# Decode attention with a dense block: a scheduled kernel of two load queues written anew as a looped program of one

## The chip, the cores and the metric

One core of one Trainium2 chip. The metric is device time in microseconds (us): the median of three runs, beside one profiled execution of the same program. PE is TensorE, DVE is VectorE, ACT is ScalarE, POOL is GpSimd, SP is SyncE; a name such as SPq stands for the engine's instruction queue. Matrix products in float32 are recorded as two passes each, so one matmul of the program is two records.

## The reference, cut to what matters

```python
B, D, H, Sk, Dh, F = 2, 512, 32, 8192, 128, 1792       # one new token for each of two sequences, float32

q = (layernorm(x) @ wq).reshape(B, 1, H, Dh)
scores = einsum("bhqd,bhkd->bhqk", q, k_cache) * Dh ** -0.5
o = einsum("bhqk,bhkd->bhqd", softmax(scores), v_cache)
h = x + o.reshape(B, 1, H * Dh) @ wo
r = relu(layernorm(h) @ w1 + b1)
out = h + (r * r) @ w2 + b2
```

There are 64 pairs of a head and a sequence. Each pair has 4 MiB of K and 4 MiB of V, and each of those bytes is used once. wq and wo have 8 MiB each, w1 and w2 3.5 MiB each.

## The kernel before

The host lays the data out so that each transfer is one row for each of the 128 partitions. K is laid with the head dimension on the partitions and the 8192 keys along the row, in two chunks (`NC`) of four quarters (`NQ`) of 1024 keys (`CS`). V is laid with 32 of the head's columns in each of four groups of partitions, so that the partition 32j + m holds quarter j, and four tiles (`NH`) of 1024 keys cover the 128 columns.

A pair has two chunks, and one chunk t goes through two steps. `front(t)`: eight matmuls (line 154) put the scores of 4 x 1024 keys into a tile `s` in PSUM, four at a time in four column groups of the array, with q repeated 32 times as the weights; DVE takes the negated maximum of each partition (line 156); ACT overwrites the scores with their exponentials and sums them (line 158). `back(t)`: DVE multiplies the exponentials with each of four tiles of V and sums along the row (line 166), writing the products themselves to a scratch tile `junk`.

The pairs lie in ten groups of heads (`GROUPS`, 4 heads down to 1). Each group has its own load of wq and wo, a projection of its q (`project_q`, line 140), a correction of its partial maxima and sums (`weigh`), and a joining step that multiplies with wo and adds into `hT` (`combine`, lines 195 to 208). At the end stand the second layer norm (`centre`), the products with W1 (line 252) and W2 (line 266), and the store.

The order of the instructions is the order in which the program calls them, two chunks ahead (`AHEAD`), and a tile framework puts in the waits: a load waits until the tile's last use is over. K, wq, wo, W1 and W2 are issued by SP (lines 57, 63, 68, 228, 232), V by ACT (line 73, and line 77 for the last but one pair); the last pair's V is issued by SP in eight pieces (line 80). There are three K tiles and two V tiles of 4 MiB (32 KiB in each partition). The loop over chunks is unrolled: 7969 instructions are in the trace.

Of the kernel before, what the change touches and what calls it, by code (L numbers as in the profile page):

```python
# [1 line left out]

# [9 lines left out]
AX = mybir.AxisListType  # L12

# [6 lines left out]
GROUPS = [4] * 7 + [2, 1, 1]  # L20
HEAD0 = [sum(GROUPS[:g]) for g in range(len(GROUPS))]
NG = len(GROUPS)
# [4 lines left out]
T = BH * NC  # L27
TH = B * NC
AHEAD = 2
W2_PIECES = [4, 4, 3, 2, 1]  # L30
# [4 lines left out]
@with_exitstack  # L35
def attention_block_kernel(ctx: ExitStack, tc: tile.TileContext, small, kd, vd, wqd, wod, w1d, w2d, out):
    nc = tc.nc
    consts = ctx.enter_context(tc.tile_pool(name="consts", bufs=1))
    kp = ctx.enter_context(tc.tile_pool(name="kp", bufs=3))
    vp = ctx.enter_context(tc.tile_pool(name="vp", bufs=2))  # L40
    wts = ctx.enter_context(tc.tile_pool(name="wts", bufs=2))
    work = ctx.enter_context(tc.tile_pool(name="work", bufs=2))
    ps_s = ctx.enter_context(tc.tile_pool(name="ps_s", bufs=3, space=bass.MemoryType.PSUM))
    ps_m = ctx.enter_context(tc.tile_pool(name="ps_m", bufs=2, space=bass.MemoryType.PSUM))


    sm = consts.tile([P, DB * B + FB + DB], F32, name="sm")
# [4 lines left out]
    KT, VT, WQ, WO = {}, {}, {}, {}  # L52

    def load_wq(g):
        n = P * DB * DH
        WQ[g] = wts.tile([P, DB, GROUPS[g] * DH], F32, name="wq")
        nc.sync.dma_start(WQ[g].rearrange("p d c -> p (d c)"),
                          wqd[HEAD0[g] * n : (HEAD0[g] + GROUPS[g]) * n].rearrange("(p x) -> p x", p=P))

    def load_wo(g):  # L60
        n = P * D
        WO[g] = wts.tile([P, GROUPS[g], D], F32, name="wo")
        nc.sync.dma_start(WO[g].rearrange("p h c -> p (h c)"),
                          wod[HEAD0[g] * n : (HEAD0[g] + GROUPS[g]) * n].rearrange("(p x) -> p x", p=P))

    def load_k(i):
        KT[i] = kp.tile([P, NC, NQ, CS], F32, name="k")
        nc.sync.dma_start(KT[i], kd[i])

    def load_v(i):  # L70
        VT[i] = vp.tile([P, NC, NH, CS], F32, name="v")
        if i < BH - 2:
            nc.scalar.dma_start(VT[i], vd[i])
            return
        for c in range(NC):
            if i < BH - 1:
                nc.scalar.dma_start(VT[i][:, c], vd[i][:, c])
            else:
                for e in range(NH):
                    nc.sync.dma_start(VT[i][:, c, e], vd[i][:, c, e])  # L80


    ones_d = consts.tile([P, P], F32, name="ones_d")
    nc.vector.memset(ones_d, 1.0 / D)
    eps_t = consts.tile([P, 1], F32, name="eps_t")
    nc.vector.memset(eps_t, EPS)
    zero = consts.tile([P, 1], F32, name="zero")
    nc.vector.memset(zero, 0.0)
    pick = consts.tile([P, NQ, P], F32, name="pick")
    nc.vector.memset(pick, 0.0)  # L90
    pick_all = consts.tile([P, P], F32, name="pick_all")
    nc.vector.memset(pick_all, 0.0)
    for j in range(NQ):
        nc.vector.memset(pick[32 * j : 32 * j + 1, j, :], 1.0)
        nc.vector.memset(pick_all[32 * j : 32 * j + 1, :], 1.0)
    ident = consts.tile([P, P], F32, name="ident")
    make_identity(nc, ident)
    fold = consts.tile([P, 32], F32, name="fold")
    nc.vector.tensor_reduce(fold, ident.rearrange("p (j m) -> p m j", j=NQ), axis=AX.X, op=ALU.add)

    def mean(src):

        part = work.tile([P, B], F32, name="part")
        nc.vector.tensor_reduce(part, src.rearrange("p d b -> p b d"), axis=AX.X, op=ALU.add)  # L104
        pm = ps_m.tile([P, B], F32, name="pm")
        nc.tensor.matmul(pm, ones_d, part, start=True, stop=True)  # L106
        return pm

    def centre(src):

        xc = work.tile([P, DB, B], F32, name="xc")
        nc.vector.tensor_tensor(xc, src, mean(src)[:, None, :].to_broadcast([P, DB, B]), op=ALU.subtract)
        sq = work.tile([P, DB, B], F32, name="sq")
        nc.vector.tensor_tensor(sq, xc, xc, op=ALU.mult)
        rstd = work.tile([P, B], F32, name="rstd")
        nc.scalar.activation(rstd, mean(sq), AF.Sqrt, bias=eps_t, scale=1.0)
        nc.vector.reciprocal(rstd, rstd)
        return xc, rstd

    load_wq(0)  # L120
    nc.sync.dma_start(sm, small)
    load_k(0)
    xn = consts.tile([P, DB, B], F32, name="xn")
    xc, rstd = centre(xT)
    nc.vector.tensor_tensor(xn, xc, rstd[:, None, :].to_broadcast([P, DB, B]), op=ALU.mult)
    hT = consts.tile([P, DB, B], F32, name="hT")
    nc.vector.tensor_copy(hT, xT)
    warm = consts.tile([P, 1], F32, name="warm")
    nc.scalar.activation(warm, eps_t, AF.Exp)


    QR, NM, LS, AC, PT, WS, RL = {}, {}, {}, {}, {}, {}, {}
    where = [(g, (hl * B + b), c) for g in range(NG) for hl in range(GROUPS[g]) for b in range(B) for c in range(NC)]

    def project_q(g):
        nb = GROUPS[g] * B
        pq = ps_m.tile([P, nb], F32, name="pm")
        for hl in range(GROUPS[g]):
            for d in range(DB):
                nc.tensor.matmul(pq[:, hl * B : (hl + 1) * B], WQ[g][:, d, hl * DH : (hl + 1) * DH], xn[:, d, :],  # L140
                                 start=(d == 0), stop=(d == DB - 1))
        QR[g] = work.tile([P, nb, 32], F32, name="qr")
        nc.vector.tensor_scalar(QR[g], pq[:, :, None].to_broadcast([P, nb, 32]), SCALE, None, op0=ALU.mult)  # L143
        NM[g] = work.tile([P, nb, NC], F32, name="nm")
        LS[g] = work.tile([P, nb, NC], F32, name="ls")
        AC[g] = work.tile([P, nb, NC, NH], F32, name="ac")

    def front(t):

        g, i, c = where[t]  # L150
        s = ps_s.tile([P, CS], F32, name="s")
        for n in range(CS // 512):
            for j in range(NQ):
                nc.tensor.matmul(s[32 * j : 32 * j + 32, n * 512 : (n + 1) * 512], QR[g][:, i, :],  # L154
                                 KT[t // NC][:, c, j, n * 512 : (n + 1) * 512], start=True, stop=True)
        nc.vector.tensor_reduce(NM[g][:, i, c : c + 1], s, axis=AX.X, op=ALU.max, negate=True)  # L156
        PT[t] = s
        nc.scalar.activation(s, s, AF.Exp, bias=NM[g][:, i, c : c + 1], scale=1.0,  # L158
                             accum_out=LS[g][:, i, c : c + 1])

    def back(t):

        g, i, c = where[t]
        for e in range(NH):
            junk = consts.tile([P, CS], F32, name="junk")
            nc.vector.scalar_tensor_tensor(junk, VT[t // NC][:, c, e, :], 1.0, PT[t], op0=ALU.mult, op1=ALU.mult,  # L166
                                           accum_out=AC[g][:, i, c, e : e + 1])

    def weigh(g):

        nb = GROUPS[g] * B
        pn = ps_m.tile([P, NQ, nb, NC], F32, name="pm")
        for j in range(NQ):
            nc.tensor.matmul(pn[:, j], pick[:, j, :], NM[g].rearrange("p i c -> p (i c)"), start=True, stop=True)  # L174
        gm = work.tile([P, nb], F32, name="gm")
        nc.vector.tensor_reduce(gm, pn.rearrange("p j i c -> p i j c"), axis=AX.XY, op=ALU.min)
        w = WS[g] = work.tile([P, nb, NC], F32, name="w")
        nc.vector.tensor_tensor(w, gm[:, :, None].to_broadcast([P, nb, NC]), NM[g], op=ALU.subtract)
        nc.scalar.activation(w, w, AF.Exp)
        if g == NG - 1:  # L180
            nc.scalar.activation(warm, w[:, 0, 0:1], AF.Sqrt)
        lw = work.tile([P, nb, NC], F32, name="lw")
        nc.vector.tensor_tensor(lw, LS[g], w, op=ALU.mult)  # L183
        pl = ps_m.tile([P, nb], F32, name="pm")
        for c in range(NC):
            nc.tensor.matmul(pl, pick_all, lw[:, :, c], start=(c == 0), stop=(c == NC - 1))  # L186
        RL[g] = work.tile([P, nb], F32, name="rl")
        nc.vector.reciprocal(RL[g], pl)

    def combine(g):  # L190

        n = GROUPS[g]
# [18 lines left out]
    for t in range(AHEAD):  # L211
        front(t)
    for t in range(T):
# [4 lines left out]
        if t == first + 1:  # L218
            load_wo(g)
# [82 lines left out]
```

## Time and profile before

| | |
|---|---|
| median of 3 runs | 1329.65 us (1328.93 to 1330.52) |
| the profiled execution, first to last instruction | 1327.8 us |
| TensorE's mean granted clock | 0.638 |
| busy: PE, DVE, ACT | 527.3, 796.6, 161.0 us |
| read from HBM | 561.00 MB |
| K loads: number, from issue to landing | 64, median 38.1 us |
| V loads: number, from issue to landing | 62, median 23.9 us |

The profiled execution's own time is its span; the median of the runs stands 1.85 us above it. A busy PE is modelled and is not PE at its peak. An engine's idle time costs nothing when another resource sets the pace. The rows of DMA tell how many of the 16 DMA engines were moving data in a stretch, and how many GB/s came of it.

### The profile page before, as it was taken

The page shows a single profiled execution, that of the slowest core. Times are in us where ns is not written, and L with a number is a line of the kernel's source. Part 1 is how long each engine was busy: PE and PEld are TensorE (multiplying, and loading weights), DVE is VectorE, ACT ScalarE, POOL GpSimd, SP SyncE. Part 2 cuts the span into 40 slices and gives each one's busy share as a digit, 9 for nine tenths or more (in the row PEclk, how much of TensorE's full clock was granted, in tenths as well). Part 3 has the DMA queues.
Part 4 walks back from the last instruction along what each step waited for, and adds up shares of the span by engine and source line. Part 5 has one row for each costly group of instructions (what it writes and reads, how often), then busy time and mean ns, then how long its engine had stood idle before and what let it go on. Part 6 is the DMA issues. An engine that isn't in the chain of part 4 may idle for free.

```text
span 1327.8 us, 7969 instructions
## 1 busy us (share of the span) xinstructions
PE 527.3 (40%) x2920; PEld 196.2 (15%) x2920; DVE 796.6 (60%) x1274; ACT 161.0 (12%) x275; POOL 0.7 (0%) x6
## 2 busy tenths in 40 slices
PE   3424345323363324523263333634235243354454
PEld 2200013000140001300030000400013000121112
DVE  1557476566456657656557646477566556557675
ACT  0111111101111111111111010111110110111111
POOL 0000000000000000000000000000000000000000
PEclk9665565666666576666676566675676666666566
DMA  9999999999999999999999999999999999999995
GB/s 407 429 427 433 428 429 434 433 430 428 431 429 434 426 430 434 429 429 433 429 431 430 430 431 431 430 434 425 433 432 430 431 429 430 433 427 435 428 398 189
DMA packets 24086, 561.58 MB, mean 423 GB/s; under 512 B 2800, under 2 KB 2928, under 8 KB 5616
## 3 DMA queue, kind: packets, MB, share of 16 engines
q1 hardware_dynamic: 14832, 296.83, 52.4%
q10 hardware_dynamic: 9216, 264.25, 46.4%
q8 instruction: 23, 0.38, 0.1%
q14 instruction: 15, 0.12, 0.0%
HBM read 561.00 MB, written 0.07 MB: 423 GB/s over the span
## 4 chain that ended last, share of the span: by engine, by line
DMA 69%; PE 14%; DVE 13%; issue 2%; another core or an unknown queue 1%; SPq 0%; DVEq 0%; ACT 0%; ACTq 0%
DMA v<-in_vd 40%; DMA k<-in_kd 27%; PE s L154 11%; DVE junk L166 11%; DMA k<-in_w1d 3%; DVE nm L156 2%; PE pm L206 1%; PE pm L140 1%; PE s L252 0%; PE s L266 0%; SPq L228 0%; PE pm L106 0%; DVEq L166 0%; ACT s L158 0%
## 5 line engine op out<-in xcount | busy, mean ns | idle before, releaser
L166 DVE SCALAR_TENSOR_TENSOR junk<-v,s 128x1024 f32<-128x1024 f32 x512 | 624.4, 1220 | 268.7 <-DMA v<-in_vd 250.5
L154 PE MATMUL s<-k,qr 128*32 128x512 f32 x2048 | 406.4, 931 | 702.4 <-DVE junk L166 551.4
L158 ACT ACTIVATE s<-s,nm 128x1024 f32<-128x1024 f32 x128 | 139.3, 1088 | 1114.6 <-DVE nm L156 1110.9
L156 DVE TENSOR_REDUCE nm<-s 128x1 f32<-128x1024 f32 x128 | 156.4, 1222 | 126.7 <-PE s L154 126.7
L154 PEld LDWEIGHTS s<-k,qr 128*32 128x32 f32 x2048 | 81.0, 146 | 1002.6 <-issue 918.9
L140 PE MATMUL pm<-xn,wq 128*128 128x2 f32 x256 | 52.7, 339 | 4.4 <-DMA wq<-in_wqd 3.6
L140 PEld LDWEIGHTS pm<-xn,wq 128*128 128x128 f32 x256 | 52.4, 315 | 5.3 <-issue 4.5
L166 DVE DVE_READ_ACCUMULATOR junk<-v,s 128x1 f32 x512 | 41.8, 82 | 0.0
L206 PE MATMUL pm<-oT,wo 128*128 128x2 f32 x256 | 36.2, 275 | 2.3 <-DVE oT L202 2.3
L206 PEld LDWEIGHTS pm<-oT,wo 128*128 128x128 f32 x256 | 35.3, 223 | 5.6 <-DVE oT L202 5.6
L143 DVE TENSOR_SCALAR qr<-pm 128x256 f32<-128x256 f32 (+2 forms) x10 | 3.7, 371 | 52.8 <-PE pm L140 52.8
L186 PE MATMUL pm<-lw,pick_all 128*128 128x8 f32 (+2 forms) x40 | 10.1, 362 | 59.1 <-DVE lw L183 59.1
L158 ACT ACTIVATION_READ_ACCUMULATOR s<-s,nm 128x1 f32 x128 | 24.7, 193 | 0.0
L202 DVE TENSOR_TENSOR oT<-pm,rl 128x8 f32<-128x8 f32 (+2 forms) x10 | 1.6, 164 | 27.8 <-PE s L154 25.5
L186 PEld LDWEIGHTS pm<-lw,pick_all 128*128 128x128 f32 x40 | 9.3, 323 | 60.0 <-DVE lw L183 51.4
L208 DVE TENSOR_TENSOR hT<-hT,pm 128x8 f32<-128x8 f32 x10 | 1.6, 163 | 26.1 <-PE pm L206 26.1
L174 PE MATMUL pm<-nm,pick 128*128 128x16 f32 (+2 forms) x80 | 11.4, 273 | 4.5 <-DVE nm L156 4.5
L174 PEld LDWEIGHTS pm<-nm,pick 128*128 128x128 f32 x80 | 10.5, 205 | 16.0 <-DVE nm L156 11.2
L106 PE MATMUL pm<-part,ones_d 128*128 128x2 f32 x8 | 2.3, 359 | 17.3 <-DVE part L104 17.3
L104 DVE TENSOR_REDUCE part<-sm 128x2 f32<-128x8 f32 x1 | 0.2, 161 | 12.8 <-DMA sm<-in_small 12.8
L200 PE MATMUL pm<-acs,fold 128*32 128x8 f32 (+2 forms) x80 | 4.4, 197 | 6.4 <-DVE acs L197 6.4
L252 PE MATMUL s<-k,xc 128*2 128x448 f32 x32 | 6.2, 749 | 0.3 <-issue 0.3
(50 smaller groups left out, 40.1 us busy)
## 6 DMA issues: line engine op xcount, KB each, us to landing
k<-in_kd SPq DMA_DIRECT2D x64, 4096.0 KB, 38.1
v<-in_vd ACTq DMA_DIRECT2D x62, 4096.0 KB, 23.9
wq<-in_wqd SPq DMA_DIRECT2D x7, 1024.0 KB, 43.1
wo<-in_wod SPq DMA_DIRECT2D x7, 1024.0 KB, 39.1
v<-in_vd ACTq DMA_DIRECT2D x2, 2048.0 KB, 12.8
v<-in_vd SPq DMA_DIRECT2D x8, 512.0 KB, 10.4
k<-in_w1d SPq DMA_DIRECT2D x4, 896.0 KB, 29.9
v<-in_w2d SPq DMA_DIRECT2D x2, 1024.0 KB, 12.4
```

Source lines behind the costliest of these rows:

```text
L106: nc.tensor.matmul(pm, ones_d, part, start=True, stop=True)
L140: nc.tensor.matmul(pq[:, hl * B : (hl + 1) * B], WQ[g][:, d, hl * DH : (hl + 1) * DH], xn[:, d, :], start=(d == 0), stop=(d == DB - 1))
L143: nc.vector.tensor_scalar(QR[g], pq[:, :, None].to_broadcast([P, nb, 32]), SCALE, None, op0=ALU.mult)
L154: nc.tensor.matmul(s[32 * j : 32 * j + 32, n * 512 : (n + 1) * 512], QR[g][:, i, :], KT[t // NC][:, c, j, n * 512 : (n + 1) * 512], start= ...
L156: nc.vector.tensor_reduce(NM[g][:, i, c : c + 1], s, axis=AX.X, op=ALU.max, negate=True)
L158: nc.scalar.activation(s, s, AF.Exp, bias=NM[g][:, i, c : c + 1], scale=1.0, accum_out=LS[g][:, i, c : c + 1])
L166: nc.vector.scalar_tensor_tensor(junk, VT[t // NC][:, c, e, :], 1.0, PT[t], op0=ALU.mult, op1=ALU.mult, accum_out=AC[g][:, i, c, e : e + 1])
L174: nc.tensor.matmul(pn[:, j], pick[:, j, :], NM[g].rearrange("p i c -> p (i c)"), start=True, stop=True)
L186: nc.tensor.matmul(pl, pick_all, lw[:, :, c], start=(c == 0), stop=(c == NC - 1))
L200: nc.tensor.matmul(po[32 * e : 32 * e + 32, :], fold, ac[:, :, e], start=True, stop=True)
L206: nc.tensor.matmul(ph[:, d, :], WO[g][:, hl, d * P : (d + 1) * P], oT[:, hl * B : (hl + 1) * B], start=(hl == 0), stop=(hl == n - 1))
L252: nc.tensor.matmul(y[32 * j : 32 * j + B, :], xc[:, d, :], W1[:, d, j * FQ : (j + 1) * FQ], start=(d == 0), stop=(d == DB - 1))
```

## The change

The kernel is written anew without the tile framework, with semaphores of its own.

- All loads but the small input go through SP's queue. K and V of one pair lie beside each other in memory, 64 KiB for each partition, and come as one load into one of three slots (`ring`). A slot is given back by DVE (`FREE`) when the pair's products are over. The 63 first pairs run in a loop of 21 rounds of three pairs on PE, DVE and ACT, and SP has a loop of its own; the addresses of sums and maxima, and of the loads, come from registers.
- wq comes whole, first, into slot 2. One step projects all of q: 32 matmuls of 512 columns with x as the weights, two transposes, and a spread of three pairs' q at a time into `qc`.
- A pair's scores wait for its K and V together. Within a pair DVE takes both maxima first, and then the eight products, which are written over V instead of over a scratch tile.
- Maxima, sums and products of all pairs stay in SBUF. The correction and the product with wo are made once for the first 62 pairs, with wo whole in slot 1 (31 matmuls of 512 columns), and once more for the last two pairs.
- The last loads come in this order: pair 62, K of pair 63, wo, V of pair 63 in five pieces, W1 in two, W2 in four. DVE adds the joined heads into `hT` after the third product of pair 63.
- W1's product takes 32 columns of weights (x repeated 16 times) instead of 2.

The core of it:

```diff
-GROUPS = [4] * 7 + [2, 1, 1]
-W2_PIECES = [4, 4, 3, 2, 1]
+HALF = NC * NQ * CS
+ROW = 2 * HALF
+W2_PIECES = [8, 4, 1, 1]
+W1_PIECES = [3, 1]
+V_PIECES = [(0, 2), (2, 4), (4, 6), (6, 7), (7, 8)]
...
+    def take(self, engine, sem, n=1):
+        engine.wait_ge(sem, n).then_inc(sem, -n)
...
+    ring = [sbuf(f"ring{s}", ROW) for s in range(3)]
...
+    load(ring[2], wqd, LD[2])
+    act.dma_start(sm, small).then_inc(SM, 16)
+    load(ring[0], kvd[0], LD[0])
+    load(ring[1], kvd[1], LD[1])
+    with sp.Fori(0, ROUNDS - 1) as r:
+        i = r * 3
+        for u in range(3):
+            t = (2 + u) % 3
+            p.take(sp, FREE)
+            load(ring[t], kvd[i + (2 + u)], LD[t])
+    p.take(sp, FREE)
+    load(ring[2], kvd[LAST - 1], LD[2])
+    p.take(sp, FREE)
+    load(ring[0][:, :HALF], kld, LK)
+    p.take(sp, FREE)
+    load(ring[1], wod, LD[1])
+    for k, (a, b) in enumerate(V_PIECES):
+        load(ring[0][:, HALF + a * CS : HALF + b * CS], vld[:, a * CS : b * CS], LV[k])
+    p.take(sp, FREE)
...
...
-    def project_q(g):
+    for n in range(2):
+        for d in range(DB):
+            for j in range(NQ):
+                c0 = d * H * DH + j * 1024 + n * 512
+                ins = pe.matmul(s[0][32 * j : 32 * j + 32, n * 512 : n * 512 + 512], xs[:, d, :], ring[2][:, c0 : c0 + 512],
+                                start=(d == 0), stop=(d == DB - 1))
...
+    def front(k, u, c, slot):
+        p.take(pe, BUFFER)
+        for n in range(CS // 512):
+            for j in range(NQ):
+                c0 = (c * NQ + j) * CS + n * 512
+                ins = pe.matmul(s[k][32 * j : 32 * j + 32, n * 512 : (n + 1) * 512], qc[:, u, :],
+                                slot[:, c0 : c0 + 512], start=True, stop=True)
+        ins.then_inc(SCORES, 1)
...
+    def product(k, pair, c, e, slot):
+        v = slot[:, HALF + (c * NH + e) * CS : HALF + (c * NH + e + 1) * CS]
+        return dve.scalar_tensor_tensor(v, v, 1.0, s[k], op0=ALU.mult, op1=ALU.mult,
+                                        accum_out=at(ac, pair, NC * NH, c * NH + e, 1))
+
+    with nc.Fori(0, ROUNDS, engines=(ENG.PE, ENG.DVE, ENG.Activation)) as r:
+        i = r * 3
+        for u in range(3):
+            if u == 0:
+                p.take(pe, QUERY)
+            p.take(pe, LD[u], 16)
+            for c in range(NC):
+                front((NC * u + c) % 3, u, c, ring[u])
+            for c in range(NC):
+                exps((NC * u + c) % 3, i + u, c)
+            for c in range(NC):
+                maxes((NC * u + c) % 3, i + u, c)
+            if u == 2:
+                dve.tensor_copy(qc, qs[:, bass.ds(i + 3, 3)][:, :, None].to_broadcast([P, 3, 32])).then_inc(QUERY, 1)
+            for c in range(NC):
+                p.take(dve, EXPED)
+                for e in range(NH):
+                    ins = product((NC * u + c) % 3, i + u, c, e, ring[u])
+                ins.then_inc(BUFFER, 1)
+            dve.drain().then_inc(FREE, 1)
...
-    def weigh(g):
-    def combine(g):
+    tok = stats(0, NG)
+    tok = sums(0, NG, tok)
+    tok = invert(0, NG, tok)
+    tok = folded(0, NG)
...
+    p.take(pe, LD[1], 16)
+    for h in range(HG):
+        j = h % NQ
+        ins = pe.matmul(pm[1][32 * j : 32 * j + 32, :], big[:, h * 32 : h * 32 + 32], WO[:, h, :],
+                        start=(h < NQ), stop=(h + NQ >= HG))
+    tok = p.tell("act", act.activation(acc, pm[1], AF.Copy))
+    for d in range(DB):
+        ins = pe.matmul(pm[0][:, d * B : (d + 1) * B], acc[:, d * P : (d + 1) * P], fold[:, :B], start=True, stop=True)
+    t_h = p.tell("pe", ins)
...
+    for n, (c, e) in enumerate(order):
+        if e == 0:
+            p.take(dve, EXPED)
+        if n in piece:
+            p.take(dve, LV[piece[n]], 16)
+        ins = product(c, LAST, c, e, ring[0])
+        if n == 2:
+            p.after("dve", t_h)
+            t_h = p.tell("dve", dve.tensor_tensor(hT, hT, pm[0][:, : DB * B].rearrange("p (d b) -> p d b", b=B), op=ALU.add))
+            t_m = t_h
+            t_w = stats(NG, B)
+        if n == 4:
+            t_l = sums(NG, B, t_w)
+            act.activation(warm, eps_t, AF.Sqrt)
+        if n == 5:
+            t_l = invert(NG, B, t_l)
```

`p.tell` counts an instruction on its engine's semaphore, and `p.after` makes an engine wait for such a count.

More of the change, by code (lines that the diff above doesn't have):

```diff
@@ L96, in attention_block_kernel @@
[L96 to L107, printed above, removed]
@@ new lines, in attention_block_kernel @@
+    p.after("dve", tok)
+    tok = p.tell("dve", dve.scalar_tensor_tensor(a2, a1, 0.0, a1, op0=ALU.max, op1=ALU.mult))
+    p.after("pe", tok)
+    at_m = 0
+    for k, n in enumerate(W2_PIECES):
+        p.take(pe, LW2[k], 16)
+        for m in range(at_m, at_m + n):
+            for j in range(NQ):
+                ins = pe.matmul(o[32 * j : 32 * j + B, :], a2[:, m, :], W2[:, m, j * P : (j + 1) * P],
+                                start=False, stop=(m == FB - 1))
+        at_m += n
+    tok = p.tell("pe", ins)
@@ L273 @@
+    p.after("dve", tok)
+    tok = p.tell("dve", dve.tensor_copy(res, o))
+    sp.wait_ge(p.done["dve"], tok[1])
+    sp.dma_start(out, res).then_inc(OUT, 16)
+    nums = sorted(x.num for x in p.sems)
+    assert nums == list(range(nums[0], nums[-1] + 1)), nums
+    sp.sem_clear(range(nums[0], nums[-1] + 1))
+    p.take(sp, OUT, 16)
 def kernel(A_x, A_k_cache, A_v_cache, A_wq, A_wo, B_x, B_w1, B_b1, B_w2, B_b2):
     import numpy as np
-    import concourse.bacc as bacc
     from concourse.bass_utils import run_bass_kernel_spmd
```

466 lines of the change are left out of this document (261 added, 205 removed).

## The prediction

> **What bounds the kernel now.** I read the page first: the span, the two bandwidth rows of the slices, the packet and HBM rows, and the head of the chain that ended last.
>
> ```profile
> span 1327.8 us, 7969 instructions
> PE 527.3 (40%) x2920; PEld 196.2 (15%) x2920; DVE 796.6 (60%) x1274; ACT 161.0 (12%) x275; POOL 0.7 (0%) x6
> ...
> DMA  9999999999999999999999999999999999999995
> GB/s 407 429 427 433 428 429 434 433 430 428 431 429 434 426 430 434 429 429 433 429 431 430 430 431 431 430 434 425 433 432 430 431 429 430 433 427 435 428 398 189
> DMA packets 24086, 561.58 MB, mean 423 GB/s; under 512 B 2800, under 2 KB 2928, under 8 KB 5616
> ...
> HBM read 561.00 MB, written 0.07 MB: 423 GB/s over the span
> ...
> DMA 69%; PE 14%; DVE 13%; issue 2%; another core or an unknown queue 1%; SPq 0%; DVEq 0%; ACT 0%; ACTq 0%
> ```
>
> The DMA engines are full in 39 of 40 slices at 425 to 435 GB/s, while the busiest compute engine, DVE, works 60% of the span. So time is bytes over rate, plus what the ends lose. The chain's 14% of PE and 13% of DVE are steps which free a tile for the next load; they cost nothing as long as another load is streaming.
>
> Then the stretches, to see the ends (columns: stretch, its length, busy time and count of PE, weight loads, DVE, ACT, POOL, granted clock, DMA share, GB/s):
>
> ```profile
> 0.00:3.00 3.00, 0.00 (x0) 0.00 (x0) 1.93 (x13) 1.28 (x1) 0.70 (x6) 1.00 0.55 164
> ...
> 40.00:1240.00 1200.00, 467.71 (x2490) 164.82 (x2493) 734.72 (x1140) 144.25 (x246) 0.00 (x0) 0.63 1.00 430
> ...
> 1284.00:1290.00 6.00, 2.18 (x27) 1.15 (x16) 5.96 (x12) 2.41 (x4) 0.00 (x0) 0.82 1.00 404
> 1290.00:1298.00 8.00, 3.64 (x16) 0.59 (x16) 5.92 (x11) 0.55 (x1) 0.00 (x0) 0.50 0.86 317
> 1298.00:1312.00 14.00, 4.71 (x28) 4.51 (x28) 10.87 (x24) 3.18 (x6) 0.00 (x0) 0.50 0.94 356
> 1312.00:1328.00 16.00, 10.96 (x158) 5.19 (x158) 2.51 (x12) 0.26 (x1) 0.00 (x0) 0.79 0.04 12
> ```
>
> There are three losses against a steady 430 GB/s. At the start 3.0 x (1 - 164/430) = 1.9 us. From 1284 to 1312 the last V tile, W1 and W2 come in many small pieces: (6 x 26 + 8 x 113 + 14 x 74)/430 = 4.9 us. From 1312 on only arithmetic is left, 16 us. 561.0 MB at 430 is 1304.7 us, and 1304.7 + 1.9 + 4.9 + 16 = 1327.5, so the account closes on the span. The median of the runs, 1329.65, stands 1.85 us above this profiled execution's 1327.8; I add that at the end.
>
> **Steady loads: one queue, 64 KiB rows.** The bytes are the same: K, V, all four weights, once each. What changes is the size of a row, one packet. Here are the queue rows of two long stretches, 100 to 1200 us and 20 to 1260 us (packets, MB, share of the 16 engines):
>
> ```profile
> DMA packets 18100, 473.48 MB, mean 430 GB/s; under 512 B 1999, under 2 KB 1999, under 8 KB 2631
> ## 3 DMA queue, kind: packets, MB, share of 16 engines
> q1 hardware_dynamic: 10266, 245.72, 52.1%
> q10 hardware_dynamic: 7802, 227.35, 48.1%
> ...
> DMA packets 20395, 533.70 MB, mean 430 GB/s; under 512 B 2255, under 2 KB 2255, under 8 KB 2895
> ## 3 DMA queue, kind: packets, MB, share of 16 engines
> q1 hardware_dynamic: 11668, 279.88, 52.6%
> q10 hardware_dynamic: 8692, 253.37, 47.6%
> ```
>
> q10 carries V alone in 32 KiB rows: 227.35 MB are 6938 rows, so 864 of its packets are semaphore writes. Of q1's 10266, 1999 - 864 = 1135 are such, and 9131 carry data, part of them small rows of wq and wo. With a fixed time a per row and b per MB: 6938a + 227.35b = 0.481 x 16 x 1100 = 8466 us and 9131a + 245.72b = 9170 us, which gives a = 12 ns. The second stretch, worked the same way, gives 2 ns. Rounding of the shares blurs each by 11 ns, so a lies between 0 and 23; I take 7, the middle of the two. The first stretch has 18100 - 1999 = 16101 data rows, 1006 an engine in 1100 us. The changed kernel has 8 rows an engine for each pair of 8.39 MB, 19.5 us: 451 in 1100 us. 555 rows saved x 7 ns = 3.9 us of 1100, 0.35%: 430 becomes 431.5 GB/s (430 with a = 0, 435 with a = 23). The Trainium skill ("DMA: Bandwidth & Descriptors", Specifications) puts a fabric ceiling at 435 GB/s; the trace's best slice, 435, agrees.
>
> All loads then end at E = 1.9 + 561.0/0.4315 = 1302 us (1306.6 with 430, 1291.6 with 435), provided that the one queue never runs dry and that the small last pieces no longer leave gaps. Both have to be shown.
>
> The ring. Rows that price one pair, and two fronts of it from the timeline (16 records are the 8 matmuls of one chunk), and the pace of products:
>
> ```profile
> L166 DVE SCALAR_TENSOR_TENSOR junk<-v,s 128x1024 f32<-128x1024 f32 x512 | 624.4, 1220 | 268.7 <-DMA v<-in_vd 250.5
> L154 PE MATMUL s<-k,qr 128*32 128x512 f32 x2048 | 406.4, 931 | 702.4 <-DVE junk L166 551.4
> L158 ACT ACTIVATE s<-s,nm 128x1024 f32<-128x1024 f32 x128 | 139.3, 1088 | 1114.6 <-DVE nm L156 1110.9
> L156 DVE TENSOR_REDUCE nm<-s 128x1 f32<-128x1024 f32 x128 | 156.4, 1222 | 126.7 <-PE s L154 126.7
> ...
> 606.64 3.64 PE L154 MATMUL s<-k,qr 128*32 128x512 f32 x16 [4.67 <-DMA k<-in_kd]
> 627.34 1.92 PE L154 MATMUL s<-k,qr 128*32 128x512 f32 x16 [1.48 <-DVE junk L166]
> ...
> 1253.83 1.22 DVE L166 SCALAR_TENSOR_TENSOR junk<-v,s 128x1024 f32<-128x1024 f32 x1 [3.03 <-DMA v<-in_vd]
> 1255.10 1.22 DVE L166 SCALAR_TENSOR_TENSOR junk<-v,s 128x1024 f32<-128x1024 f32 x1
> ...
> 1325.40 0.35 SPq L270 DMA_DIRECT2D out<-res  x1
> ```
>
> One chunk's scores take 406.4/128 = 3.17 us on average (1.92 to 3.64 by the granted clock). A pair in the ring starts when K and V have both landed: two chunks of scores 6.3, the second maximum 1.2 (the first, and both exponentials, lie beside scores and products, but for about 1), eight products at 1.27 = 10.2. That is 19 us until the slot is given back. The load for that slot is due when the next two pairs have landed, 2 x 19.4 = 39 us after it: 20 us of cover. Writing products over V costs the same as writing them to the scratch tile: both write 128x1024 in SBUF. Addresses from registers add an instruction ahead of each product, maximum and exponential, not shown in this trace; between 0 and 0.35 us each (the issue on SP is the nearest row), at most 4.2 us a pair, covered. SP waits with nothing behind it but these loads in the order in which slots come free. At the start, Wq lands at 1.9 + 19.5 = 21.4; 32 matmuls of 512 columns are four chunks, 12.7 us, then two transposes and the spread of q, 3 us by allowance; its slot is free at 37, and pair 1 lands at 60. If its small input on ACT's queue shares each engine row by row, it comes by 8 x 2.4 = 19 us, still ahead of Wq. So no wait reaches the queue. The group projections and joins that leave PE and DVE in the middle are worth nothing, because the loads hid them.
>
> **The end.** In the new order Wo lies ahead of V63, W1, W2: 11.53 MB, 27 us, so Wo lands at E - 27. The joint sums of 62 pairs are done by then: pair 62 lands 24.1 MB before the last byte, at E - 56, and is finished at E - 37; K63's maxima and the sums take some 10. From Wo on there is a chain that has not been on the path before:
>
> ```profile
> L206 PE MATMUL pm<-oT,wo 128*128 128x2 f32 x256 | 36.2, 275 | 2.3 <-DVE oT L202 2.3
> L246 ACT ACTIVATE s<-zero 128x448 f32<-128x448 f32 x1 | 0.5, 547 | 9.6 <-DVE junk L166 9.6
> ...
> 1308.09 1.22 DVE L166 SCALAR_TENSOR_TENSOR junk<-v,s 128x1024 f32<-128x1024 f32 x1
> ...
> 1310.44 1.87 PE L206 MATMUL pm<-oT,wo 128*128 128x2 f32 x8 [0.27 <-DVE oT L202]
> ```
>
> Landing seen by PE 1, an allowance; 31 matmuls of 512 columns, four at a time like the scores, 31/8 x 3.17 = 12.3 (7.4 to 14.1); the copy on ACT 0.8 (512 columns to 448 in 0.55, and a hand-over); four matmuls against 128x128 weights 1.6 (8 records of L206 took 1.87 late); hT 0.3; only now DVE goes on past product 2 (the addition into hT waits in its queue, and five products stand behind it): four pick matmuls 1.7, two small vector steps 0.4, five products with two small steps between 6.5. The sum is 24.6, so the last product ends at E - 27 + 24.6 = E - 2.4, though its V landed at E - 17. From there the steps are those of before, where the last product ended at 1308.09 + 1.22 = 1309.3 and the span at 1327.8: 18.5 us. (32 columns of weights instead of 2 change no matmul's length, and one copy is new, 0.2.) W2's last piece, at E, is covered. End = E + 16 (E + 11 to E + 18 by the matmuls' bounds). The 4.9 us of gaps go, since nothing on SP waits between the last eleven issues; their small rows cost 0.6.
>
> Sum: 1302 + 16 = 1318 for the span, plus 1.85: **1319.5 us**, 10 us or 0.8% less. Against before: -3.9 x 1.2 (rows), -4.9 (gaps), and the end neither gains nor loses.
>
> **The rivals.**
> Rows of 64 KiB are moved as two of 32, or a is 0: E = 1306.6, time 1306.6 + 16 + 1.85 = 1324.5. For it: 2 ns in one stretch. Against: 12 in the other.
>
> A costlier row and a full clock at the end: a = 23, E = 1291.6, and the end at E + 14 gives 1307. The blur allows it; the clock of 0.63 over the run speaks against.
>
> Slower, by the memory: with 64 KiB rows the sixteen engines read twice as far apart, and they may meet in the same part of the memory. It decides from 561.0/(1329.65 - 1.85 - 16 - 1.9) = 428.3 GB/s down. The lowest rate with full engines above is 404 (1284 to 1290): 561.0/0.404 + 1.9 + 16 + 1.85 = 1408; 1% under 430 gives 1337. Against it: rows of 8 to 32 KiB all fit one a and b. The Trainium skill (same page, Latency and other measured facts, "HBM row pitch at large powers of two") has copies fall from 214 to 207 GB/s at a pitch of 512 KiB between partitions and further beyond. No run here shows a pitch as large; those 3% taken off 431.5 would make it about 1364.
>
> Slower, by the ring: if a pair holds its slot for more than 37 us instead of 19, the queue runs dry, and each us beyond costs a third of one in each of 63 pairs, 21 us: 40 us would give 1383. Nothing in the rows comes near it, but the loop's branch and its register steps have no row.
>
> **How the numbers follow.** Forecast 0.60 (1313 to 1323 by the clock and a), rows for nothing 0.15, costlier rows 0.08, memory 0.09, ring 0.05, no change 0.03. The range runs from 1307 to 1328, which leaves the two slow cases, 0.14, out. A measurement can tell 0.2%, 2.7 us: faster (below 1327) 0.82, same 0.04, slower 0.14.
>
> **What would show it.** Right: the slices at 431 to 432 GB/s up to some 40 us before the end, one data queue, and about 11,300 packets instead of 24,086; the chain's last 40 us going from Wo's landing through the 31 matmuls to the output; DVE busy some 60%. The row term fails if the slices stay at 430; the ring fails if SP's waits are followed by slices below 9; the end fails if the last product ends well before the loads do, or more than 18 us lie between the last load and the end. A rate below 428 makes the whole forecast wrong.

## The result, and the profile after

| | before | after |
|---|---|---|
| median | 1329.76 us (1328.93 to 1330.52) | 1310.4 us (1309.21 to 1312.31) |
| profiled execution: span | 1327.8 us | 1309.7 us |
| ratio, with its 95% interval | | 0.9854 (0.984 to 0.9868) |

The change takes 19.4 us off, 1.5%. The forecast was 10 us, 1319.5 with a range of 1307 to 1328. The page of the kernel after, cut to the rows that answer to those of before:

```profile
span 1309.7 us, 8250 instructions
PE 410.1 (31%) x2390; PEld 112.6 (9%) x2390; DVE 759.0 (58%) x1227; ACT 160.2 (12%) x267; POOL 0.7 (0%) x6
...
DMA  9999999999999999999999999999999999999996
GB/s 417 417 447 422 442 438 426 444 422 444 420 444 420 446 418 446 420 444 436 428 444 420 446 420 444 420 444 420 446 418 446 428 436 442 422 444 422 430 423 271
DMA packets 11381, 561.14 MB, mean 428 GB/s; under 512 B 1392, under 2 KB 1520, under 8 KB 2160
...
q8 instruction: 3, 0.05, 0.0%
```

The DMA engines are still full in 39 of 40 slices, and DVE still works 58% of the span, so the same resource is the bound. The slices now go up and down between 417 and 447, because the profile counts a packet's bytes where the packet starts: in a slice of 32.7 us an engine starts 13 or 14 rows of 64 KiB, which is 416 or 448 GB/s. Their mean is what matters. It stands in the stretches, with the end beside it (columns as in the prediction):

```profile
0.00:3.00 3.00, 0.00 (x0) 0.00 (x0) 1.78 (x13) 0.00 (x0) 0.70 (x6) 1.00 1.05 350
...
40.00:1200.00 1160.00, 347.42 (x1920) 87.57 (x1920) 696.87 (x1097) 144.55 (x240) 0.00 (x0) 0.63 1.00 433
...
1296.00:1298.00 2.00, 1.44 (x9) 0.45 (x12) 0.63 (x4) 0.00 (x0) 0.00 (x0) 0.50 0.85 318
1298.00:1300.00 2.00, 2.00 (x16) 0.67 (x12) 0.00 (x0) 0.00 (x0) 0.00 (x0) 0.50 0.12 47
1300.00:1304.00 4.00, 3.18 (x26) 0.90 (x18) 1.12 (x5) 0.26 (x1) 0.00 (x0) 0.71 0.00 0
```

433 GB/s stands where 430 stood. The 350 GB/s of the first 3 us, for 164 before, are this way of counting and no gain: 1.05 MB is one row of 64 KiB on each of the 16 engines. With each packet's bytes spread over the packet's own time, 16.17 MB had come by 40 us and 16.09 in the kernel before, 0.2 us apart. At the end all sixteen engines run out together within some 2 us, near 1298.5. The ring's pace is seen in the timeline of pair 61, from its first scores to the issue of Wo, which goes into its slot:

```profile
1224.25 5.10 PE L239 MATMUL s<-ring,qc 128*32 128x512 f32 x32 [13.10 <-PEq L61]
...
1237.66 1.22 DVE L254 SCALAR_TENSOR_TENSOR ring<-ring,s 128x1024 f32<-128x1024 f32 x1
...
1238.80 1.22 DVE L254 SCALAR_TENSOR_TENSOR ring<-ring,s 128x1024 f32<-128x1024 f32 x1
...
1240.16 0.33 SPq L123 DMA_DIRECT2D ring<-in_wod  x1
```

The pair holds its slot for 1240.2 - 1224.3 = 16 us, where 19 were forecast and 39 are there. Two products follow each other in 1.14 us. The end, from the matmuls with Wo to the store:

```profile
1272.52 9.99 PE L344 MATMUL pm<-ring,big 128*32 128x512 f32 x62 [2.42 <-PEq L61]
1282.55 0.60 ACT L348 ACTIVATE acc<-pm 128x512 f32<-128x512 f32 x1 [16.18 <-PE pm L344]
...
1284.29 0.16 DVE L366 TENSOR_TENSOR hT<-hT,pm 128x8 f32<-128x8 f32 x1 [5.59 <-PE pm L351]
...
1290.87 1.22 DVE L254 SCALAR_TENSOR_TENSOR ring<-ring,s 128x1024 f32<-128x1024 f32 x1
...
1308.08 0.35 SPq L428 DMA_DIRECT2D out<-res  x1
```

This is the new chain of the forecast: Wo, 31 matmuls, the copy, the addition into hT for which DVE idles 5.59 us, five products to 1292.1, and from there 17.6 us to the end of the span.

The places that the forecast names are all there, yet 9 us more are gone than its terms give. Where the unforecast half comes from is the question of the experiments.

### The profile page after: what moved, and what is told of

The parts are those of the page before. It is cut to its first block, busy times and chain, and to the rows that moved or that the text cites. A ratio compares the mean times of both kernels' runs of the same rounds, so it can differ in the third digit from the quotient of the medians.

```text
span 1309.7 us, 8250 instructions
## 1 busy us (share of the span) xinstructions
PE 410.1 (31%) x2390; PEld 112.6 (9%) x2390; DVE 759.0 (58%) x1227; ACT 160.2 (12%) x267; POOL 0.7 (0%) x6
## 5 line engine op out<-in xcount | busy, mean ns | idle before, releaser
L239 PE MATMUL s<-ring,qc 128*32 128x512 f32 x2048 | 369.8, 888 | 852.0 <-PEq L61 852.0
L254 DVE SCALAR_TENSOR_TENSOR ring<-ring,s 128x1024 f32<-128x1024 f32 x512 | 589.5, 1217 | 3.7 <-DVEq L61 3.6
L245 DVE TENSOR_REDUCE nm<-s 128x1024 f32 (+1 forms) x128 | 156.7, 1225 | 488.4 <-DVEq L61 488.4
L239 PEld LDWEIGHTS s<-ring,qc 128*32 128x32 f32 x2048 | 93.0, 155 | 1128.5 <-issue 1128.5
L254 DVE DVE_READ_ACCUMULATOR ring<-ring,s (+1 forms) x512 | 42.5, 83 | 0.0
L249 ACT ACTIVATION_READ_ACCUMULATOR s<-s,nm (+1 forms) x128 | 24.7, 193 | 0.0
L344 PE MATMUL pm<-ring,big 128*32 128x512 f32 x62 | 10.0, 798 | 2.4 <-PEq L61 2.4
L216 PE MATMUL s<-ring,xr 128*32 128x512 f32 x64 | 9.7, 773 | 2.3 <-issue 2.3
L180 PE MATMUL pm<-part,ones_d 128*128 128x2 f32 x4 | 1.2, 363 | 23.6 <-DVE part L178 23.6
L396 PE MATMUL s<-ring,xr 128*32 128x448 f32 x32 | 5.9, 886 | 0.6 <-issue 0.6
L291 PEld LDWEIGHTS pm<-nm,pick 128*128 128x128 f32 x16 | 2.9, 271 | 5.7 <-DVE hT L285 5.4
```

Source lines behind the costliest of these rows:

```text
L216: ins = pe.matmul(s[0][32 * j : 32 * j + 32, n * 512 : n * 512 + 512], xs[:, d, :], ring[2][:, c0 : c0 + 512], start=(d == 0), stop=(d == ...
L239: ins = pe.matmul(s[k][32 * j : 32 * j + 32, n * 512 : (n + 1) * 512], qc[:, u, :], slot[:, c0 : c0 + 512], start=True, stop=True)
L245: dve.tensor_reduce(at(nm, pair, NC, c, 1), s[k], axis=AX.X, op=ALU.max, negate=True).then_inc(MAXED, 1)
L249: act.activation(s[k], s[k], AF.Exp, bias=at(nm, pair, NC, c, 1), scale=1.0, accum_out=at(ls, pair, NC, c, 1)).then_inc(EXPED, 1)
L254: return dve.scalar_tensor_tensor(v, v, 1.0, s[k], op0=ALU.mult, op1=ALU.mult, accum_out=at(ac, pair, NC * NH, c * NH + e, 1))
L291: ins = pe.matmul(pm[0][:, j * nb * NC : (j + 1) * nb * NC], pick[:, j, :], nm[:, n2], start=True, stop=True)
```

## The experiments

Each ratio is against the kernel before, run on the same chip beside it. A difference in us is between medians; where no other kernel is named, it is to the changed kernel's 1309.13 of the second measurement, which comes first here. The two measurements of the changed kernel stand 1.3 us apart (1310.4 and 1309.13), so a difference of 1 us between kernels that were not run beside each other is noise.

**The change once more, as a base for the others.**

> The changed kernel once more, unchanged, as the base for the runs beside it: 0.985 of the kernel before, about 1310 us, 433 GB/s in the middle.

Measured: 1309.13 us (1308.90 to 1310.34), ratio 0.9847 (0.9833 to 0.986).

**Rows of 32 KiB.** K and V of a pair as two loads, still on one queue.

```diff
+    def load_pair(t, src):
+        for a in (0, HALF):
+            load(ring[t][:, a : a + HALF], src[:, a : a + HALF], LD[t])
-            load(ring[t], kvd[i + (2 + u)], LD[t])
+            load_pair(t, kvd[i + (2 + u)])
-            p.take(pe, LD[u], 16)
+            p.take(pe, LD[u], 32)
```

> Each pair's 64 KiB rows come as two loads of 32 KiB rows on the same queue, K first, and the scores wait for both; nothing else changes. My theory, a fixed time of some 8 ns for each row, says 504 more rows an engine, so 4 to 5 us more than the changed kernel (about 1315) and 431.5 GB/s in the middle instead of 433. The rival that the rows are worth the whole step from 430 to 433 GB/s says 9 us more (1319). The rival that one queue instead of two made the step says no change (1310).

Measured: 1314.74 us, ratio 0.9885 (0.987 to 0.99): 5.6 us slower than the change. Packets and bytes from 100 to 1200 us, after first, then this kernel:

```profile
DMA packets 8164, 476.19 MB, mean 433 GB/s; under 512 B 898, under 2 KB 898, under 8 KB 898
```

```profile
DMA packets 16304, 474.96 MB, mean 432 GB/s; under 512 B 1809, under 2 KB 1809, under 8 KB 1809
```

Twice as many data rows (14495 for 7266) carry 0.26% less in the same time. That share is coarse, since one row of 64 KiB on each engine is 1.05 MB. With each packet's bytes spread over its own time, the two kernels move 433.5 and 431.8 GB/s here, 0.39%, which is 5.1 us of 1300. The row term is real: 504 more rows an engine for 5.6 us are 11 ns each, where 7 was taken.

**Two queues.** As the last one, with V issued by ACT as in the kernel before.

```diff
+        if more:
+            p.take(act, VFREE)
+            act.dma_start(ring[t][:, HALF:], kvd[i + (u + 2)][:, HALF:]).then_inc(LD[t], 16)
```

> As the run with 32 KiB rows, but the V half of each pair is issued by ACT on its own queue, right after the exponentials of the pair two before it, when its slot has long been free. The theory of rows says the same time as with 32 KiB rows on one queue, within 1 us, and 431 GB/s. The rival that two queues cost something by themselves says 430 GB/s or less and another 4 us or more.

Measured: 1314.54 us, ratio 0.9888 (0.9873 to 0.9903), 0.2 us from the kernel of 32 KiB rows. One queue or two makes no difference that can be told from noise. The Trainium skill ("DMA: Bandwidth & Descriptors", Issuing engines are not separate DMA queues) says that transfers of different issuers run on the same 16 engines and interleave; these two medians agree.

**The loops unrolled.** The same work in the same order, with constant addresses and no loop on any engine.

```diff
-    with sp.Fori(0, ROUNDS - 1) as r:
+    for r in range(ROUNDS - 1):
-        return tile[:, bass.ds(pair * n + off, size)]
+        return tile[:, pair * n + off : pair * n + off + size]
-    with nc.Fori(0, ROUNDS, engines=(ENG.PE, ENG.DVE, ENG.Activation)) as r:
+    for r in range(ROUNDS):
```

> The changed kernel with both loops unrolled and fixed addresses, all else the same. My theory says that loops bring no time by themselves, since every wait of a pair is covered: only some twenty 16 KiB blocks of instructions more to fetch, 0 to 2 us slower (1310 to 1312). The rival that the loops are a good part of the gain, through the fetching of instructions that holds up single DMA engines, says 4 us or more (1314 and up). The rival that register steps and branches cost time says that it becomes faster, by 1 us or more.

Measured: 1318.96 us, ratio 0.992 (0.9906 to 0.9933): 9.8 us slower than the change, so the expectation of 0 to 2 fell. The unrolled kernel's queue rows, and its stretches:

```profile
q8 instruction: 19, 0.31, 0.1%
q14 instruction: 16, 0.13, 0.0%
```

```profile
40.00:1200.00 1160.00, 346.63 (x1920) 90.40 (x1920) 687.27 (x1082) 142.78 (x237) 0.00 (x0) 0.63 1.00 433
...
1300.00:1304.00 4.00, 1.43 (x14) 1.34 (x14) 2.33 (x7) 0.00 (x0) 0.00 (x0) 0.50 0.17 68
1304.00:1308.00 4.00, 2.99 (x18) 1.80 (x21) 0.95 (x6) 0.00 (x0) 0.00 (x0) 0.50 0.06 24
```

The middle is about as fast as in the looped kernel, 433 GB/s. The end is not: a DMA share of 0.06 is one engine in sixteen. By the packets' records its last data come at 1308.8 us, and those of the other fifteen between 1297.6 and 1302.2. Seen closer, in this kernel from 1302 to 1309 us, and in the kernel before from 1312 to 1316:

```profile
DMA packets 36, 0.18 MB, mean 26 GB/s; under 512 B 5, under 2 KB 5, under 8 KB 23
```

```profile
DMA packets 30, 0.11 MB, mean 27 GB/s; under 512 B 5, under 2 KB 5, under 8 KB 29
```

433/16 is 27 GB/s: both are the stream of a single engine. What the unrolled program has and the looped one lacks is instructions to fetch, 19 + 16 blocks on two queues instead of 3 (shown above) + 2, and they go through the DMA engines. The kernel before has as many:

```profile
q8 instruction: 23, 0.38, 0.1%
q14 instruction: 15, 0.12, 0.0%
```

A load is complete when its slowest engine is, so the products of the last pairs, Wo's matmuls (1282.26 instead of 1272.52) and everything behind them came 9.7 us later.

**V, W1 and W2 in the pieces of before.** No wait is added on SP.

```diff
-W2_PIECES = [8, 4, 1, 1]
-W1_PIECES = [3, 1]
-V_PIECES = [(0, 2), (2, 4), (4, 6), (6, 7), (7, 8)]
+W2_PIECES = [4, 4, 3, 2, 1]
+W1_PIECES = [1, 1, 1, 1]
+V_PIECES = [(k, k + 1) for k in range(8)]
```

> The changed kernel with the last V in eight pieces of 4 KiB rows, W1 in four pieces and W2 in five, the sizes of the kernel before, but issued without a wait between them. If the 4.9 us that the kernel before lost between 1284 and 1312 us came from SP's waits, the loads end at most 1 us later and the time stays within 1 us of the changed kernel. If the small rows themselves were slow, the loads end 3 to 5 us later, and the time rises by 1 to 4 us.

Measured: 1309.28 us, ratio 0.9853 (0.9838 to 0.9868): nothing. Small pieces by themselves cost no time.

**The join behind the last product.** The addition into hT and the statistics of the last two pairs come after all eight products.

```diff
-        if n == 2:
-            p.after("dve", t_h)
...
-        if n == 5:
-            t_l = invert(NG, B, t_l)
+    p.after("dve", t_h)
...
+    t_l = invert(NG, B, t_l)
```

> The addition of the joined heads into hT, and the maxima, sums and inverses of the last two pairs, stand behind all eight products of pair 63 instead of between them. If the product with Wo and what hangs on it paces the end, the products now end near their V's landing, some 8 us earlier, the steps behind Wo come without five products between them, and the time falls by 3 to 5 us. If the end hangs on V's landing or on W2's, nothing changes.

Measured: 1306.64 us, ratio 0.983 (0.9816 to 0.9843): 2.6 us less than the kernel in pieces, which was run beside it and is as fast as the change; 3 to 5 were expected. DVE's queue behind that wait is on the path, as the prediction had it: in the profiled runs the last product ends 5.9 us earlier. The steps moved behind the products take back a part: from there to the end it is 22.1 us instead of 17.6.

**The statistics early.** The last two pairs' maxima and sums are joined beside those of the 62, in a bank of their own, and only the addition into hT follows the products.

```diff
-    tok = stats(0, NG)
-    tok = sums(0, NG, tok)
+    tok = stats(0, NG, pm[0])
+    t_w = stats(NG, B, e0)
+    tok = sums(0, NG, tok, pm[1])
+    t_l = sums(NG, B, t_w, e1)
```

> As the run before, and the maxima, sums and inverses of the last two pairs are taken ahead of the product with Wo, in columns of a PSUM tile that is free by then. My theory says that Wo's chain is then 11 us shorter, the last W2 piece becomes the bound, and the end comes 3 to 4 us after the loads' end instead of 12: 8 to 9 us less than the changed kernel, about 1301.5. The rival that the last matmuls and the store need their 17 us after the products whatever stands ahead says 3 to 5 us less, as for the run before.

Measured: 1303.94 us (1303.85 to 1304.19), ratio 0.981 (0.9797 to 0.9824), the fastest of all kernels here, 5.3 us below the kernel in pieces. The last product and the store of this kernel:

```profile
1283.79 1.22 DVE L254 SCALAR_TENSOR_TENSOR ring<-ring,s 128x1024 f32<-128x1024 f32 x1
...
1301.02 0.35 SPq L425 DMA_DIRECT2D out<-res  x1
```

Its span is 1302.6, 17.6 us after the last product, as in the changed kernel. The rival, that the end follows the last product whatever stands ahead, was right, and the 8 to 9 us fell: the products ended 5.7 us earlier than in the profiled run of the kernel in pieces, and so did the span.

**Products to a scratch tile, with a wait between them.** Each product waits for the one before it, as a scratch tile shared by all makes it do.

```diff
-                    ins = product((NC * u + c) % 3, i + u, c, e, ring[u])
-                ins.then_inc(BUFFER, 1)
+                    product((NC * u + c) % 3, i + u, c, e, ring[u], big).then_inc(JUNK, 1)
+                    p.take(dve, JUNK)
+                dve.sem_inc(BUFFER, 1)
```

> The changed kernel with the products of the looped pairs written to one scratch tile, each product waiting for the one before it through a semaphore, instead of over V. The trace after shows products every 1.14 us where the kernel before had one every 1.26 us. If the wait of DVE for its own last write makes that difference, the products come every 1.25 us or more here, and the time stays within 1 us of the changed kernel, since the loads hide 1 us a pair. If the place written matters by itself and not the wait, the pace stays at 1.14 us. If a pair's time in its slot matters, the time rises by some us.

Measured: 1311.46 us, ratio 0.9867 (0.9852 to 0.9883), about 2 us more than the change and the kernel in pieces, where at most 1 was expected. It is near the edge of the noise: its runs, 1310.5 to 1312.3, lie above those of the second measurement of the change and inside those of the first. Two products of this kernel:

```profile
600.98 1.22 DVE L255 SCALAR_TENSOR_TENSOR big<-ring,s 128x1024 f32<-128x1024 f32 x1 [0.24 <-DVEq L61]
...
602.45 1.22 DVE L255 SCALAR_TENSOR_TENSOR big<-ring,s 128x1024 f32<-128x1024 f32 x1 [0.24 <-DVEq L61]
```

They take 1.47 us from start to start instead of 1.14, and one product itself stays at 1.22. The wait and the other place, which were changed together, cost 0.33 each, and 504 of them, 166 us of DVE, cost about 2 us of time: the loads go on at 433 GB/s beside them, and what is left is that the last looped pair's products end 2 us later. That the place itself, the scratch tile or V, matters is not seen in the 1.22 us of a product; it was not tried without the wait.

**Only PE unrolled.** DVE, ACT and SP keep their loops.

```diff
-    with nc.Fori(0, ROUNDS, engines=(ENG.PE, ENG.DVE, ENG.Activation)) as r:
+    for r in range(ROUNDS):
...
+    with nc.Fori(0, ROUNDS, engines=(ENG.DVE, ENG.Activation)) as r:
```

> The changed kernel with the loop unrolled for PE alone; DVE, ACT and SP keep theirs. The unrolled kernel was 9.8 us slower than the looped one, against my theory of 0 to 2. My new theory: PE's instructions come in 16 KiB blocks through the same DMA engines (19 in the unrolled trace, about 1 us each, against 3), they fall on one or two engines, those fall behind the others, and each load waits for its last engine. It says that PE alone brings 7 to 9 of the 9.8 us: about 1317. The rival that straight code is slow for DVE, ACT or SP says at most 2 us, about 1310.

**Only DVE, ACT and SP unrolled.** PE keeps its loop.

```diff
-    with sp.Fori(0, ROUNDS - 1) as r:
+    for r in range(ROUNDS - 1):
-    with nc.Fori(0, ROUNDS, engines=(ENG.PE, ENG.DVE, ENG.Activation)) as r:
+    with pe.Fori(0, ROUNDS):
...
+    for r in range(ROUNDS):
```

> The other half: PE keeps its loop, DVE, ACT and SP are unrolled with fixed addresses. Their blocks are 8 KiB and took 5 us in all in the unrolled trace. The theory of fetched blocks says 0 to 2.5 us slower than the changed kernel, 1309 to 1312. The rival says 8 us or more.

Measured: 1312.33 us, ratio 0.9873 (0.9857 to 0.989), for PE alone, and 1320.45 us, ratio 0.9933 (0.9917 to 0.995), for the others: 3 and 11 us over the change, the 3 close to the noise. I had it the wrong way round, by the number of bytes. Of the kernel with only PE unrolled, then of the other:

```profile
q8 instruction: 19, 0.31, 0.1%
...
q14 instruction: 2, 0.02, 0.0%
```

```profile
q14 instruction: 17, 0.13, 0.0%
q8 instruction: 3, 0.05, 0.0%
```

So q8's blocks, of 0.31 MB/19 = 16 KiB, are PE's, and q14's, 16 of 8 KiB and one packet of 80 bytes, belong to one or more of the others. The smaller ones do the harm. How it grows shows in the time at which SP issues the same load, K of pair 63, in the changed kernel and in the one with the others unrolled:

```profile
1221.91 0.34 SPq L123 DMA_DIRECT2D ring<-in_kld  x1
```

```profile
1230.20 0.33 SPq L123 DMA_DIRECT2D ring<-in_kld  x1
```

At about 100 us the two kernels' issues are 0.4 us apart, at about 410 they are 1.3 apart, here 8.3. The lag gathers slowly over the whole run.

The single packets' records in these traces show how it gathers. They do not name a packet's DMA engine, but a packet starts within 20 ns of the end of the one before it on its engine, so each engine can be followed. In the kernel with DVE, ACT and SP unrolled, 12 of the 16 blocks stand on one and the same engine, 100 or 115 us apart. A block itself takes 0.31 to 0.33 us, which is what its bytes need at 27 GB/s. The row of 64 KiB behind it takes 3.05 to 3.08 us, where the median row takes 2.42. That is 0.98 us a block and 11.8 us for the twelve. This engine brings its last data at 1309.1 us, the other fifteen theirs by 1300.5. The last data of the changed kernel come at 1299.4, 9.7 us earlier, so this lag is nearly all of the 11 us.

A block of PE costs more, 1.0 to 1.1 us and some 0.5 for the row behind it. But with PE unrolled these blocks are spread over nine engines, mostly two on each. Two are 3.1 us, and eight engines end some 3 us behind the others: these are the 3 us. So the number of blocks on the worst engine counts, and not their sum. The fully unrolled kernel fits this: it has both kinds of block, and its last data come at 1308.8, no later than here.

Between two of the twelve blocks the trace has 128 instructions of DVE on average (119 to 138), 33 of ACT and 11 of SP, so they look like DVE's; no run unrolls DVE alone. Why the row behind a block takes longer stays open.

**All three parts of before at once.** Two queues of 32 KiB rows and all engines unrolled, with the start and the end of the change.

> Rows of 32 KiB, V on ACT's queue and all loops unrolled, together; the start, the one join and the order of the last loads stay as in the changed kernel. If the parts add, it takes 1309.1 + 5.6 + 9.8 = 1324.5, 5 us less than the kernel before, and that rest is the start and the end. If the parts overlap (two queues let the engine that lags catch up), it takes 1316 to 1321, and the rest is larger.

Measured: 1324.53 us (1323.37 to 1325.68), ratio 0.9962 (0.9948 to 0.9976). The single effects add up: 1309.1 + 5.6 - 0.2 + 9.8 = 1324.3. To the 1329.42 of before there remain 4.9 us for what else differs: the start, the weights' loads in the middle and the end. The start has next to nothing of it: with bytes spread as above, 16.18 MB had come by 40 us and 16.09 in the kernel before. By 1200 us it was 516.1 MB and 514.9, 2.7 us; between them the kernel before has the small rows of its ten groups' wq and wo, which no run tests.

**Waits on SP between the last loads.** The kernel with early statistics and the pieces of before, in which SP issues a piece only when the fourth before it has landed.

```diff
+    def four_back(n):
+        if n >= 4:
+            sp.wait_ge(TAIL[n - 4], 16)
```

> The kernel with the early maxima and sums (1303.9), its last loads in pieces of the old sizes, and SP issues each of them only when the one four places before it has landed, as the kernel before had its issues held. Without waits the small pieces cost nothing. If such waits by themselves made the 4.9 us of gaps, the loads end 3 to 5 us later and the time is 1306 to 1309. If the gaps came from one DMA engine that lagged, which here does not lag, the waits cost 1 us at most, and the time is 1303.5 to 1305.

Measured: 1306.35 us, ratio 0.9827 (0.9811 to 0.9844), 2.4 us over the kernel with early statistics: by the time, the low end of the first expectation. From 1240 to 1290 us, early statistics first, then with waits:

```profile
1240.00:1290.00 50.00, 30.68 (x188) 14.72 (x192) 29.61 (x59) 7.51 (x14) 0.00 (x0) 0.67 0.98 418
```

```profile
1240.00:1290.00 50.00, 31.97 (x192) 14.40 (x192) 30.07 (x59) 7.51 (x14) 0.00 (x0) 0.67 0.98 407
```

The waits take 11 of 418 GB/s over 50 us, 1.3 us of loading, and the last data come 1.4 us later, at 1301.1 for 1299.7, where that expectation had 3 to 5. This price can't be carried over to the kernel before, where one engine lags. There the last data come at 1316.3, in the kernel of all three parts, which has no such waits, at 1314.9: 1.5 us in the two profiled runs, for all that differs in the loads. These runs' spans differ by 3.4, so 1.9 us lie behind the last data. How the 4.9 us divide is not shown beyond that.

## Why the prediction was right, and what it missed

| part | forecast, us | measured, us |
|---|---|---|
| rows of 64 KiB | -4.6 | -5.6 |
| two queues to one | 0 | 0 (0.2) |
| loops in place of an unrolled program | 0 | -9.8 |
| gaps at the end, start, small weights' rows, rest of the end | -4.9, all as gaps | -4.9 together; at most 1.5 by an earlier end of the loads, in the profiled runs |
| products over V | 0 | 0 (a wait between products would cost 2) |

**The bound and the direction** were right: bytes over rate plus the ends, before and after. That the time fell into the range is in good part luck. The low end, 1307, was set by a costlier row and a full clock, while half of the gain came from a step that the forecast put at nothing. The sum has a slip too: 1302 + 16 + 1.85 is 1319.85 and not 1319.5, and the 0.6 for small rows is not in it.

**Rows.** a = 7 ns gave 431.5 GB/s; the stretch has 433, and the single test gave 5.6 us, 11 ns a row. So the mechanism held, and the middle of 2 and 12 ns was too low. The forecast's 555 rows in 1100 us are some 660 of the run; the 150 of them that the test leaves out would be another 1.7 us at 11 ns each, an estimate that no run tests.

**The gaps.** Small pieces alone cost nothing. SP's waits between them cost 2.4 us where no engine lags. That the remainder of 4.9 us equals the forecast's 4.9 is chance: with the gaps gone, in the kernel of all three parts, the last data came only 1.5 us earlier. So I read the dim stretches of before from 1284 to 1312 as engines that run dry while the program waits for the one of the next paragraph, and such idleness costs little.

**The failed step** is the one on the loop: it priced the addresses from registers, noted that the loop's branch and register steps have no row, and so looked only for what a loop adds. It had no term for what an unrolled program costs. The rows for it were in the page of before, q8 23 blocks and q14 15, at shares of 0.1% and 0.0% which look like nothing. So was its effect: the prediction took the 0.04 of DMA share after 1312 for no transfer and wrote that "only arithmetic is left", where one engine was still bringing W2. 561.0 MB at 430 GB/s and 1.9 for the start end at 1306.6, and the last engine of before ended near 1316: 9.4 us, about the 9.8 of the unrolled loops. The account still closed on the span, because those 9.4 us were booked elsewhere: 4.9 as gaps, and 4.5 within the 16 us of arithmetic, of which 1327.8 - 1316 = 11.8 are left. The changed kernel has about as many, 11.

On this step a rule of the Trainium skill ("Runtime: NRT & Kernel Launch", Instruction fetch mechanics) differs from the runs: crossing an instruction block is called "mostly hidden", and full unrolling is what kernels prefer, since a taken branch can stall the fetch. Here 63 pairs unrolled cost 9.8 us, and the loop's own stalls do not show beside 433 GB/s of loads. The measurement decides: what the fetch cost stands on the DMA engine that brought the blocks, and the loads waited for that engine. Whether the engines that execute also waited does not show, since DVE is idle for 42% of the span and the others for more.

**Ring, query projection, small input.** 16 us of hold for 19; the small input came at 22.98 us for 19, behind rows of 64 KiB; Q's projection took 9.67 us for 12.7, so the slot was free near 38 us, 37 forecast, and pair 1 was still landing. That 38 is so near 37 is luck: the layer norm ahead of the projection, 4.3 us from 22.98 to 27.29, had no term, and the shorter matmuls made up for it.

**The end.** The loads ended near 1298.5 for E = 1302. The chain from Wo's matmuls to the last product took 1292.1 - 1272.5 = 19.6 us, the same steps forecast at 23.6; the 31 matmuls 9.99 for 12.3, and most of the others were also a little shorter. From the last product 17.6 us for 18.5. The end came some 11 us after the loads instead of 16. The median stands only 0.7 above the profiled execution's span, not 1.85, since that execution was the slowest of the four. By the table the loops were worth 9.8 us more than forecast and the rows 1.0: 10.8 in all, the 20.3 between the kernels where they were compared part by part, less the 9.5 of the forecast's terms.

**The rivals.** Rows for nothing fell with 5.6 us. The memory rival fell: 64 KiB rows ran at 433 GB/s, above the 428.3 from which it decides; whether the larger pitches that the prediction cites from the Trainium skill would slow them, no run here shows. The ring rival fell with a DMA share of 1.00. A costlier row came nearest to the time, for another reason.

## What to carry to other kernels

A mean over sixteen DMA engines hides the one that lags. Look for a share near 1/16 behind the apparent end of the loads, and read the instruction queues' rows with it: in a kernel bound by loads, which wait for the slowest engine, a loop can be worth more than larger rows: here 9.8 us for 5.6. Take care with the GB/s of short stretches: a row counts where it starts, and with 64 KiB rows one on each engine is 1.05 MB. What stands behind the last load is worth an order of its own: moving two small joins off it gave 5 us more.

## What the runs showed of the hardware that was not expected

- An instruction block holds its DMA engine for longer than its bytes need: with the 8 KiB blocks, the block takes 0.32 us and the 64 KiB row behind it 0.66 us more than others. Twelve of them on one engine made the program 11 us slower. PE's blocks of 16 KiB cost some 1.55 us each, but lay mostly two to an engine: 3 us. Together it was 9.8, not the sum, since loads wait for the slowest engine.
- A product that waits for the one before it on its own engine starts 1.47 us after it instead of 1.14, though each is shown with the same 1.22.
- 64 KiB rows against 32 KiB rows: 5.6 us of 1310 on one core, and 0.2 us between one queue and two.
